# The last row group of the last down projection by column halves, each half added and stored on its own

## Chip, cores, metric

One core of one Trainium2 chip. The metric is the device time of the whole program in microseconds (us). The change acts on the last 4 us, so a second measure is used, the **tail**: from the start of the last matmul to the end of the span, read from the records of a trace.

## The reference

```python
x = A_u                                                    # [1, 2048, 640], bf16
h = x + _A_ref(_layernorm(x), ...)                         # a long convolution; not touched
h2 = h + _B_ref(_layernorm(h), B_w_gate, B_w_up, B_w_down) # 640 -> 1728 -> 640

def _B_ref(x, w_gate, w_up, w_down):
    g = jnp.einsum("bsd,df->bsf", x, w_gate)
    u = jnp.einsum("bsd,df->bsf", x, w_up)
    return jnp.einsum("bsf,fd->bsd", _sigmoid(g) * u, w_down)
```

## The kernel before

The sequence is worked on in four blocks (`b`) of 512 rows, each as four row groups (`lr`) of 128. For each block the down projection runs over two pairs of row groups (`lp` 0 and 2, `k` 0 and 1). A row group's 640 output columns are two halves (`c`) of 320, each in a PSUM bank. The two halves are slices of **one** tile `[P, 2, 512]`. In the last block the halves are added to `h` straight from PSUM and the row group is stored at once.

```python
        for lp in (0, 2):
            # ... (another pool setting, not in use)
                po = [[t[:, c] for c in range(2)] for t in (pso_p.tile([P, 2, 512], F32, name="ml_po", tag="ml_po") for _ in range(2))]

            def chunks(k, start, stop):
                lr = lp + k
                for ft in range(FT):                       # FT = 13
                    for c in range(2):
                        nc.tensor.matmul(po[k][c][:, 0:320], lhsT=hm[:, ft, 128 * lr:128 * lr + 128], rhs=Wd[:, ft, 320 * c:320 * c + 320],
                                         start=(start and ft == 0), stop=(stop and ft == FT - 1))
            # ... chunks(0), then the last 64 rows of both row groups side by side, then chunks(1)
            for k in range(2):
                lr = lp + k
                hv = hs[b][:, lr, :]
                h2 = hv.rearrange("p (c w) -> p c w", c=2)
                for c in range(2):
                    # ... (blocks 0 to 2 evict with ScalarE first)
                    nc.vector.tensor_tensor(h2[:, c], tb if b < NB - 1 else po[k][c][:, 0:320], h2[:, c], ALU.add)
                if b == NB - 1:
                    nc.sync.dma_start(oh[b, :, lr:lr + 1, :], hs[b][:, lr:lr + 1, :])
```

## Time and profile before

| | before |
|---|---|
| time | 356.66 us median of the first three runs (356.56 to 356.86) |
| span of the profiled run, granted clock | 355.0 us, 0.995 |
| tail | 3.87 us |

In the records of the trace, counted from the start of the last matmul, the tail goes like this: the first addition starts at 0.34, the second at 0.74, the store is issued at 1.25, its landing is seen at 3.05, the list of closing semaphore waits ends at 3.12, and the closing barriers take another 0.75. The prediction below shows the lines of the profile and how to read them.

### The profile page before, as it was taken

What the parts mean: (1) busy time and instruction counts of PE and PEld (TensorE: products, weight loads), DVE (VectorE), ACT (ScalarE), POOL (GpSimd) and SP (SyncE); (2) the same over time, 40 slices, a digit from 0 to 9 for tenths busy, and PEclk for the clock granted to TensorE, in tenths of its full rate; (3) what the DMA queues carried; (4) which work ended last, traced back from release to release, by engine and by line L of the source; (5) the groups of instructions that cost most, each with busy time, mean ns of one, the idle gap of its engine ahead of it and who ended that gap; (6) DMA issues with size and microseconds to landing.
All of it is one profiled execution on the core that took longest, in us unless ns stands there. A gap on an engine that the chain in (4) does not pass through costs nothing.

```text
span 355.0 us, 6617 instructions
## 1 busy us (share of the span) xinstructions
PE 320.4 (90%) x2584; PEld 204.0 (57%) x2584; DVE 283.3 (80%) x570; ACT 245.9 (69%) x455; POOL 11.4 (3%) x20
## 2 busy tenths in 40 slices
PE   2587989997799999899999899998899999999995
PEld 1464667765487778755456554555554456544463
DVE  3899999999898799879999899999899951211222
ACT  6999999998999764673767845547844678455500
POOL 1020002200000000100000100000100001000000
PEclk9998999999999999999999999999999999999999
DMA  6990000454205339989500053000012000400011
GB/s 172 323 404 4 15 2 2 113 179 157 76 3 160 137 88 352 289 273 280 227 4 0 5 179 113 3 0 0 3 74 76 0 1 11 133 7 1 0 37 38
DMA packets 32391, 35.00 MB, mean 99 GB/s; under 512 B 19676, under 2 KB 27741, under 8 KB 32104
## 3 DMA queue, kind: packets, MB, share of 16 engines
q1 hardware_dynamic: 32360, 34.59, 30.7%
q8 instruction: 20, 0.33, 0.4%
q14 instruction: 11, 0.09, 0.1%
HBM read 24.70 MB, written 9.21 MB: 96 GB/s over the span
## 4 chain that ended last, share of the span: by engine, by line
DVE 28%; PE 18%; issue 14%; ACT 2%; POOL 1%; POOLq 0%; DVEq 0%; ACTq 0%
DVE u L694 5%; PE ml_po L942 5%; DVE u L693 5%; PE ml_pg L909 5%; PE ml_pu L909 4%; DVE u L696 3%; DVE u L697 3%; DVE ml_hm L920 2%; DVE VR L704 2%; PE ps_y L565 1%; DVE Z L673 1%; DVE y L701 1%; DVE y L702 1%; DVE h L805 1%; ACT ln L859 1%
## 5 line engine op out<-in xcount | busy, mean ns | idle before, releaser
L909 PE MATMUL ml_pg<-lnT,Wg 128*128 128x512 bf16 x260 | 64.6, 379 | 0.2 <-ACT ml_sg L917 0.2
L909 PE MATMUL ml_pu<-lnT,Wu 128*128 128x512 bf16 x260 | 64.4, 379 | 0.0
L942 PE MATMUL ml_po<-Wd,ml_hm 128*128 128x320 bf16 x416 | 59.5, 299 | 1.7 <-ACT Wd L963 1.7
L942 PEld LDWEIGHTS <-ml_hm 128*128 128x128 bf16 x416 | 40.1, 98 | 19.6 <-issue 3.7
L917 ACT ACTIVATE ml_sg<-ml_pg 128x512 bf16<-128x512 f32 x52 | 30.9, 597 | 25.5 <-PE ml_pg L909 11.9
L920 DVE TENSOR_TENSOR ml_hm<-ml_ub,ml_sg 128x512 bf16<-128x512 bf16 x52 | 22.0, 423 | 28.0 <-ACT ml_ub L919 28.0
L909 PEld LDWEIGHTS <-Wu 128*128 128x128 bf16 x260 | 25.4, 98 | 30.7 <-issue 0.3
L919 ACT CAST ml_ub<-ml_pu 128x512 bf16<-128x512 f32 x52 | 30.4, 584 | 17.0 <-PE ml_pu L909 16.9
L909 PEld LDWEIGHTS <-Wg 128*128 128x128 bf16 x260 | 25.4, 98 | 28.8 <-issue 0.4
L457 PE MATMUL ps_z<-u,c_G 128*128 128x320 bf16 x192 | 30.3, 307 | 4.5 <-ACT zs L458 2.7
L518 PE MATMUL ps_xk<-kv,c_KM 128*128 128x160 bf16 x320 | 27.0, 232 | 1.8 <-ACT S L522 0.8
L693 DVE TENSOR_TENSOR u<-Z,S 128x1280 bf16<-128x1280 bf16 x34 | 27.8, 820 | 0.0
L694 DVE TENSOR_TENSOR u<-Z,S 128x1280 bf16<-128x1280 bf16 x34 | 27.8, 820 | 0.0
L457 PEld LDWEIGHTS <-c_G 128*128 128x128 bf16 x192 | 18.9, 99 | 13.7 <-issue 6.0
L518 PEld LDWEIGHTS <-c_KM 128*128 128x128 bf16 x320 | 23.5, 98 | 4.5 <-issue 3.5
L247 PE MATMUL ps_t<-fr,c_dg 128*128 128x160 f16 (+1 forms) x180 | 19.7, 240 | 4.9 <-DMA c_dg<-s4c_dg 4.1
L247 PEld LDWEIGHTS <-c_dg 128*128 128x128 f16 x180 | 14.9, 100 | 11.4 <-DMA c_dg<-s4c_dg 4.7
L697 DVE TENSOR_TENSOR u<-u,u 128x1280 bf16<-128x1280 bf16 x23 | 18.9, 821 | 0.1
L696 DVE TENSOR_TENSOR u<-u,u 128x1280 bf16<-128x1280 bf16 x23 | 18.9, 821 | 0.0
L476 PE MATMUL pk<-tabB,tabA 128*128 128x84 bf16 x320 | 16.1, 200 | 1.8 <-ACT kts L477 1.4
L477 ACT CAST kts<-pk 128x420 bf16<-128x420 f32 x32 | 15.9, 558 | 1.8 <-PE pk L476 1.8
L476 PEld LDWEIGHTS <-tabA 128*128 128x128 bf16 x320 | 14.3, 97 | 4.8 <-issue 3.3
(158 smaller groups left out, 546.1 us busy)
## 6 DMA issues: line engine op xcount, KB each, us to landing
dz<-zs SPq DMA_DIRECT2D x12, 320.0 KB, 2.4
c_KM<-s4c_KM SPq DMA_DIRECT2D x1, 2560.0 KB, 12.6
dxk<-xk SPq DMA_DIRECT2D x16, 160.0 KB, 3.8
h<-in_A_u_dram SPq DMA_DIRECT2D x4, 640.0 KB, 4.4
eo<-dz SPq DMA_DIRECT2D x4, 640.0 KB, 4.3
S<-dxk SPq DMA_DIRECT2D x4, 640.0 KB, 5.3
Wg<-in_B_w_gate_dram SPq DMA_DIRECT2D x4, 520.0 KB, 9.4
Wu<-in_B_w_up_dram SPq DMA_DIRECT2D x4, 520.0 KB, 8.5
```

The source lines that it names most:

```text
L247: MM(ps[:, a, q * w:q * w + w], lhsT=dg[:, dk, :], rhs=fr[:, src, i, o + oo:o + oo + w], start=False, stop=(q == m - 1 and i == 1))
L457: MM(ps[:, ri, 0:UH], lhsT=G[:, ft, 0 if b in EO else hf, ri, r, :], rhs=us[b][:, r, o:o + UH], start=(r == rr[0]), stop=(r == rr[-1]))
L476: MM(pk[:, i, :], lhsT=A[:, ri, g].rearrange("p e c -> p (e c)"), rhs=B[:, ri, :, 4 * g:4 * g + 4], start=(ri == 0), stop=(ri == 1))
L518: mm = MM(ps[:, hf, ri * W:ri * W + W], lhsT=KM[:, ft, hf, ri, KI[d] + q, :], rhs=kv[:, j, :], start=(q == 0), stop=(q == len(KD[d]) - 1)).ins
L693: V(t1, z, k[:, :, :, hs_], ALU.mult)
L694: V(t2, z, k[:, :, ::-1, hs_], ALU.mult)
L696: V(s1, s1, t1, ALU.add)
L697: V(s2, s2, t2, ALU.add)
L909: nc.tensor.matmul(ps[:], lhsT=W[:, dc, f0:f0 + 128], rhs=lnT[:, dc].rearrange("p a b -> p (a b)"), start=(dc == 0), stop=(dc == 4))
L917: nc.scalar.activation(sg[:], pg[:], AF.Sigmoid)
L919: nc.scalar.copy(ub[:], pu[:])
L942: nc.tensor.matmul(po[k][c][:, 0:320], lhsT=hm[:, ft, 128 * lr:128 * lr + 128], rhs=Wd[:, ft, 320 * c:320 * c + 320], start=(start and ft ...
```

## The change

The intent: the matmuls of the very last row group first complete the left 320 columns and then the right ones, so that the left half can be added and stored beside the right half's 13 matmuls. The core of the diff (the rest moves code into a function and adds branches for a setting that is not in use):

```diff
+            end = b == NB - 1 and lp
+
             def chunks(k, start, stop):
                 lr = lp + k
-                for ft in range(FT):
-                    for c in range(2):
-                        nc.tensor.matmul(...)
+                for ft, c in [(ft, c) for c in range(2) for ft in range(FT)] if end and k else [(ft, c) for ft in range(FT) for c in range(2)]:
+                    nc.tensor.matmul(...)
@@
                     nc.vector.tensor_tensor(h2[:, c], ...)
-                if b == NB - 1:
+                    if end and k:
+                        nc.sync.dma_start(oh[b, :, lr, 320 * c:320 * c + 320], hv[:, 320 * c:320 * c + 320])
+                if b == NB - 1 and not (end and k):
                     nc.sync.dma_start(oh[b, :, lr:lr + 1, :], hs[b][:, lr:lr + 1, :])
```

More of the change, by code (lines that the diff above doesn't have):

```diff
@@ L869, in turn @@
             return
-        if b and AT["PW"]:
+        if b and AT["PW"] == 1:
             pts = [pso[0].tile([P, 4, 4, 128], BF16, name="ml_pt", tag="ml_po") for _ in range(2)]
@@ L878, in turn @@
         for dc in range(5):
-            pt = psg_p.tile([P, 4, 128], BF16, name="ml_pt", tag="ml_pg")
+            pp, tag = (pso[1], "ml_pu") if b and AT["PW"] == 2 else (psg_p, "ml_pg")
+            pt = pp.tile([P, 4, 128], BF16, name="ml_pt", tag=tag)
             for i in range(4):
@@ L895, in mlp @@
     pso_p = sc.pool("ml_pso", bufs=2, space=PSUM)
-    pso.append(pso_p)
+    pso += [pso_p, psu_p]
     tc.cur_priority += int(AT["LATER"])
@@ L909, in up, with last_up @@
                 nc.tensor.matmul(ps[:], lhsT=W[:, dc, f0:f0 + 128], rhs=lnT[:, dc].rearrange("p a b -> p (a b)"), start=(dc == 0), stop=(dc == 4))
+        def last_up():
+            pg = psg_p.tile([P, 512], F32, name="ml_pg", tag="ml_pg")
+            for dc in range(5):
+                nc.tensor.matmul(pg[:], lhsT=Wl[:, dc].rearrange("p a b -> p (a b)"), rhs=lnT[:, dc].rearrange("p a b -> p (a b)"), start=(dc == 0), stop=(dc == 4))
+            sg = tmp.tile([P, 512], BF16, name="ml_sg")
+            nc.scalar.activation(sg[64:128, :], pg[0:64, :], AF.Sigmoid)
+            for k in range(2):
+                ev = lambda t: t.rearrange("p (a b c) -> p a b c", b=2, c=128)[:, :, k]
+                nc.vector.tensor_tensor(ev(hm[64 * k:64 * k + 64, FT, :]), ev(pg[64:128, :]), ev(sg[64:128, :]), ALU.mult)
         for ft in range(FT):
@@ L922, in mlp @@
                 drain(inv, 1)
-        pg = psg_p.tile([P, 512], F32, name="ml_pg", tag="ml_pg")
-        for dc in range(5):
-            nc.tensor.matmul(pg[:], lhsT=Wl[:, dc].rearrange("p a b -> p (a b)"), rhs=lnT[:, dc].rearrange("p a b -> p (a b)"), start=(dc == 0), stop=(dc == 4))
-        sg = tmp.tile([P, 512], BF16, name="ml_sg")
-        nc.scalar.activation(sg[64:128, :], pg[0:64, :], AF.Sigmoid)
-        for k in range(2):
-            ev = lambda t: t.rearrange("p (a b c) -> p a b c", b=2, c=128)[:, :, k]
-            nc.vector.tensor_tensor(ev(hm[64 * k:64 * k + 64, FT, :]), ev(pg[64:128, :]), ev(sg[64:128, :]), ALU.mult)
-        for lp in (0, 2):
-            if lp and AT["PW"]:
+        last_up()
+        for lp in (0, 2):
+            if lp and AT["PW"] == 2:
+                po = [[psg_p.tile([P, 512], F32, name="ml_po", tag="ml_pg") for _ in range(2)]]
+                t = pso_p.tile([P, 2, 512], F32, name="ml_po", tag="ml_po")
+                po.append([t[:, c] for c in range(2)])
+            elif lp and AT["PW"]:
                 po = [[p.tile([P, 512], F32, name="ml_po", tag=t) for _ in range(2)] for p, t in ((psg_p, "ml_pg"), (psu_p, "ml_pu"))]
@@ L936, in mlp @@
                 po = [[t[:, c] for c in range(2)] for t in (pso_p.tile([P, 2, 512], F32, name="ml_po", tag="ml_po") for _ in range(2))]
+            end = b == NB - 1 and lp
             def chunks(k, start, stop):
                 lr = lp + k
-                for ft in range(FT):
-                    for c in range(2):
-                        nc.tensor.matmul(po[k][c][:, 0:320], lhsT=hm[:, ft, 128 * lr:128 * lr + 128], rhs=Wd[:, ft, 320 * c:320 * c + 320],
+                for ft, c in [(ft, c) for c in range(2) for ft in range(FT)] if end and k else [(ft, c) for ft in range(FT) for c in range(2)]:
+                    nc.tensor.matmul(po[k][c][:, 0:320], lhsT=hm[:, ft, 128 * lr:128 * lr + 128], rhs=Wd[:, ft, 320 * c:320 * c + 320],
                                          start=(start and ft == 0), stop=(stop and ft == FT - 1))
```

## The prediction

> **What bounds the kernel now.** I read the page first, then the chain of waits over the last microseconds, then the timeline of the end, the waits of VectorE and of the store queue there, and last the list of DMA issues.
>
> The page says that this is a TensorE kernel, at full clock, and that nothing near the end disturbs it:
>
> ```profile
> span 355.0 us, 6617 instructions
> PE 320.4 (90%) x2584; PEld 204.0 (57%) x2584; DVE 283.3 (80%) x570; ACT 245.9 (69%) x455; POOL 11.4 (3%) x20
> PEclk9998999999999999999999999999999999999999
> ```
>
> The change touches only what happens after the last gate and up matmuls, so the whole-span shares say little. What counts is the chain that ends last, in its final five microseconds:
>
> ```profile
> 349.91 1.51 PE ml_po L942 x11
> 351.42 0.02 issue
> 351.44 0.49 DVE h L964
> 351.94 0.40 DVEq L1027
> ```
>
> The last matmul of the down projection ends at 351.42, and only then does VectorE begin on the last row group: one addition of 0.49 us and a second one whose end comes 0.40 us after it. The timeline of the end shows the same two additions as one entry, and the last store behind them:
>
> ```profile
> 347.70 3.71 PE L942 MATMUL ml_po<-Wd,ml_hm 128*128 128x320 bf16 x26
> 351.44 0.89 DVE L964 TENSOR_TENSOR h<-ml_po,h 128x320 bf16<-128x320 f32 x2 [2.75 <-PE ml_po L942]
> 352.36 0.33 SPq L966 DMA_DIRECT2D out_dram<-h  x1
> ```
>
> The bracket is the line to look at: VectorE sat idle for 2.75 us before the pair, waiting for TensorE. So VectorE has plenty of time to add the first column half early, if it were told that it is ready. The views of line L966 and of the last waits give the rest:
>
> ```profile
> DMA to landing us min/median/max: 1.8/1.8/2.3
> SPq L1027 <- DMA out_dram<-h: 1.1, 1, 1.1
> ```
>
> The tail after the last matmul is therefore: 0.02 wait, 0.89 of additions (to 352.33), 0.03 to the store's issue (352.36), 1.8 to its landing (about 354.2), and 0.8 of closing barriers to 355.0. That is 3.6 us, 1% of the span. No change confined to this tail can move the time by 2%, which is 7.1 us.
>
> **What the Trainium skill says.** (1) "PSUM — Partial Sum Buffer", section "Summary: rules for kernel authors", tells a kernel that wants to read PSUM while a matmul runs to aim at a different bank and to guard by bank. The output tile here is two halves of 512 f32 each, which that page's specifications give as one bank each, so the early addition is allowed; the trace of before has no such overlap within a row group. (2) "TensorE: Matmul & The Clock Gate", section "The mechanism", says that matmuls end strictly in the order of issue, so that one increment on the last is sound. The reverse matters here: who waits for the last one's increment waits for all. The trace agrees with it in so far as both additions of before follow the last matmul by 0.02 us. (3) "DMA: Bandwidth & Descriptors", section "Anatomy of one DMA — SWDGE (gpsimd) path", puts about 2.0 us of fixed cost on a DMA, mostly the receipt of the write, plus bytes over 436 GB/s. The trace agrees in form: a store of 160 KB lands in 1.8 us, and the view of the whole-block stores (L968, 640 KB) gives 2.9 us. The slope is 1.1 us for 480 KB (0.0023 us per KB, about 447 GB/s), and the fixed part 1.8 - 160 x 0.0023 = 1.43 us; smaller than the page's, on a queue of another kind. (4) The same page's "Specifications" ask for 512 B or more per transfer for the full rate. Before has runs of 1280 B per partition, the change 640 B, still above.
>
> **The change part by part.** Everything outside the last block's second pair of row groups is the same. I compared the two built programs instruction by instruction with source lines stripped: ACT and POOL are identical, TensorE has the same 5126 instructions of which only the last 26 loads and matmuls are in another order, VectorE has the same two additions, and the store queue has two instructions more. The new branches for other pool settings are dead, as the setting is still 0.
>
> *Matmuls.* Before, the 26 matmuls alternate between the halves; after, 13 go to the first and 13 to the second. The same 26 weight loads remain. Alternation or not should not matter: line L909 puts five matmuls in a row into one bank and takes 1.08 us for five in the chain, 216 ns for 512 columns, 0.42 ns a column; L942 alternates and takes 3.53 us for 26 (the first group in the chain), 136 ns for 320 columns, also 0.42 ns. So 0.0 us, and the last matmul still ends at 351.42.
>
> *Additions.* The intent is that the first half's addition runs beside the second half's 13 matmuls. The built program says it does not. In both programs only the very last matmul of this pair of halves increments TensorE's semaphore for this tile (by 27, to 2564), and the first half's addition waits for 2564 in both; the second half's addition waits for nothing of TensorE. If the wait followed each half, the second addition would need a wait of its own. It has none, so the dependence is held for the whole two-bank tile. The first addition therefore starts at 351.44 again, and the second at 351.85, 0.41 us later. Gain 0.0 us.
>
> *Stores.* The first half's store may now go after the first addition: 351.44 + 0.49 + 0.03 = 351.96, instead of 352.36. Its issue takes 0.33 us and then one small semaphore instruction (17 ns by the view of L966), so the queue is free at 352.31, just before the second addition's end at 352.33. The second store is issued at 352.36, the time of the only store before. It carries 80 KB in place of 160, so by the slope it lands 80 x 0.0023 = 0.18 us earlier. The first store's data begin 0.4 us earlier than before and take some 0.2 to 0.3 us, so they are off the engines as the second's begin. Smaller pieces do not scale perfectly, so I take 0.15 us of gain.
>
> *Closing waits.* At the end the queue goes through a list of semaphore waits. Before, the last store's semaphore is in the last of them; after, the second store uses another one, which stands third of six, with three more after it. The view of the closing line has these at 28 ns median each, so 3 x 0.028 = 0.08 us are walked after the landing instead of before it. Loss 0.08 us.
>
> Sum: 0.0 + 0.0 - 0.15 + 0.08 = -0.07 us. From the median of 356.66, 356.6 us.
>
> **The rivals.**
> *A: the addition is hidden after all*, because I misread the wait. Then 0.41 us of additions go from the tail and the second store is issued at about 351.95; with its smaller size the gain is 0.41 + 0.15 - 0.08 = 0.5 us, and the time 356.2. For it: the 2.75 us of idle VectorE, and the two halves in two banks. Against it: the wait values of the built program, which the hardware can't pass early. I give it 4%.
> *B: the second store is held up by the first*, in the issue or in the queue, where both are in flight together with twice the pieces. If the queue is late by a tenth or the first store's last writes have to be confirmed before the second's, the landing comes 0.1 to 0.4 us later than I said: 356.7 to 356.9. For it: the margin at the issue is only 0.02 us by the arithmetic above, and one of the four stores of L966 took 2.3 us to land without another in flight. Against it: the second half moves few bytes, and three of the four took 1.8. I give 25% to a result above 356.7 from this.
> *C: thirteen matmuls in a row into one bank are slower* than alternating ones. If each lost 10 ns, 26 x 0.01 = 0.26 us, and 356.9. Against it stands the equal time per column of L909 and L942. 3%.
>
> **Range and chances.** The mechanisms span 356.2 to 356.9; the three runs of before lie within 0.3 us of each other, and another set of runs may sit a few tenths off. That gives 356.2 to 357.0 for eight times in ten, centre 356.6. For 2% either way the time would have to leave 349.5 to 363.8, far outside what a 3.6 us tail can do; what is left is a surprise elsewhere in the program, though its instructions are the same. Faster 0.005, same 0.99, slower 0.005.
>
> **What would show each step right or wrong.** In the profile after, VectorE's last pair of additions should still be one entry of about 0.89 us behind the last matmul, with an idle time of about 2.75 us before it: then the split of the additions did nothing. If instead one addition stands near 349.6 (half way through the 26 matmuls) and a single one behind the last, rival A holds. The last 26 matmuls should take 3.7 us; 4.0 would be rival C. The store queue should show two issues 0.40 us apart, the second 0.94 us after the last matmul, with a landing of about 1.65 us against 1.8; 1.8 or more is rival B. From the last landing to the end of the span should be about 0.9 us instead of 0.8. The prediction is wrong if the time leaves its range, or if the first addition starts before the last matmul ends.

## The result

The changed kernel took 356.97 us (median of four runs, 356.35 to 357.59), the kernel before 356.62 us (four runs, 356.56 to 356.86). The ratio, 1.0008, has a 95% interval from 0.9989 to 1.0028: **the same**. Ratios in this text are not quite the ratio of the medians quoted.

The page of the changed kernel, its first lines and its clock line:

```profile
span 354.5 us, 6619 instructions
PE 320.6 (90%) x2584; PEld 205.0 (58%) x2584; DVE 283.4 (80%) x570; ACT 245.8 (69%) x455; POOL 11.4 (3%) x20
PEclk9999999999999999999999999999999999999999
```

The span is 0.43 us shorter than before. That is not a gain of the change: its chain of waits, over the end, shows that all of it was there before the last matmul ended (351.42 before, 350.96 now):

```profile
347.31 3.65 PE ml_po L951 x26
350.96 0.02 issue
350.98 0.49 DVE h L973
351.47 0.40 DVEq L1038
```

After that point the chain has the same pieces as before, to 0.01 us: matmuls 3.65, wait 0.02, an addition of 0.49, and the second addition's 0.40. The timeline of the end of the changed kernel:

```profile
350.98 0.89 DVE L973 TENSOR_TENSOR h<-ml_po,h 128x320 bf16<-128x320 f32 x2 [2.75 <-PE ml_po L951]
351.50 0.81 SPq L975 DMA_DIRECT2D out_dram<-h  x2
```

Both additions still stand behind the last matmul, and VectorE was idle for the same 2.75 us before them, although the left half's last matmul had started 13 matmuls earlier. Only the store has changed: two issues in 0.81 us. Their landing time, from the view of the store's line, and the semaphore waits of the closing line, first of the changed kernel:

```profile
DMA to landing us min/median/max: 1.6/1.6/1.6
L1038 SPq EVENT_SEMAPHORE  x8: 17/28/1097, 352.4 to 354.5; - x8
```

and of the kernel before:

```profile
L1027 SPq EVENT_SEMAPHORE  x8: 17/28/28, 352.7 to 354.9; - x8
```

In this view the three numbers are the shortest, median and longest duration in ns. The 1097 ns is the wait for the last store, now inside an entry that has further ones behind it.

In the records of the traces, from the last matmul's start, the landing of the last store is seen at 2.92 us (3.05 before), the list of closing waits ends at 3.15 (3.12), and the span at 3.90 (3.87). The smaller store brings 0.13 us, the list takes 0.16 us back, and the tail is 0.03 us longer.

### The profile page after: what moved, and what is told of

Read it like the earlier page. It is cut to its first block, busy times and chain, and to the rows that moved or that the text cites. A ratio compares the mean times of both kernels' runs of the same rounds, so it can differ in the third digit from the quotient of the medians.

```text
span 354.5 us, 6619 instructions
## 1 busy us (share of the span) xinstructions
PE 320.6 (90%) x2584; PEld 205.0 (58%) x2584; DVE 283.4 (80%) x570; ACT 245.8 (69%) x455; POOL 11.4 (3%) x20
## 4 chain that ended last, share of the span: by engine, by line
DVE 26%; PE 16%; issue 15%; SPq 3%; DMA 2%; ACT 1%; POOL 1%; POOLq 0%; DVEq 0%; ACTq 0%
DVE u L694 5%; PE ml_po L951 5%; DVE u L693 5%; PE ml_pg L910 5%; PE ml_pu L910 4%; DVE u L696 3%; DVE u L697 3%; DVE ml_hm L931 2%; DMA Wl<-in_B_w_gate_dram 2%; DVE VR L704 2%; SPq L822 2%; SPq L823 1%; DVE Z L673 1%; DVE y L701 1%; DVE y L702 1%
## 5 line engine op out<-in xcount | busy, mean ns | idle before, releaser
L457 PE MATMUL ps_z<-u,c_G 128*128 128x320 bf16 x192 | 29.2, 298 | 4.8 <-ACT zs L458 1.9
```

What stands on the lines that cost most here:

```text
L457: MM(ps[:, ri, 0:UH], lhsT=G[:, ft, 0 if b in EO else hf, ri, r, :], rhs=us[b][:, r, o:o + UH], start=(r == rr[0]), stop=(r == rr[-1]))
```

## The experiments

Nine runs were made, all with correct results: the first four on one chip with eleven runs of the kernel before, the next four on another chip with eleven new runs of it, and uneven_lastsem on that second chip too, with one more (its comparison uses all twelve). Each row of the table below comes from one trace; the tail of a kernel is compared, not its time, unless timed runs are quoted. A kernel without timed rounds has a single execution, whose state is unknown. All positions are us from the start of the last matmul, read from the traces' records; "landing seen" is where the wait for the last store's semaphore is over, "closing list ends" where the instruction behind the list starts.

| kernel | matmuls | PSUM tiles of the last row group | stores of it | 1st addition starts | 2nd starts | last store issued | landing seen | closing list ends | tail |
|---|---|---|---|---|---|---|---|---|---|
| before | alternate | one | 1 | 0.34 | 0.74 | 1.25 | 3.05 | 3.12 | 3.87 |
| after | halves | one | 2 | 0.34 | 0.75 | 1.28 | 2.92 | 3.15 | 3.90 |
| after_again | halves | one | 2 | 0.34 | 0.74 | 1.29 | 2.93 | 3.16 | 3.91 |
| order_only | halves | one | 1 | 0.34 | 0.75 | 1.26 | 3.05 | 3.12 | 3.87 |
| store_only | alternate | one | 2 | 0.34 | 0.75 | 1.29 | 2.93 | 3.16 | 3.92 |
| two_tiles | halves | two | 2 | -1.43 | 0.34 | 0.86 | 2.45 | 2.62 | 3.38 |
| two_tiles_one_store | halves | two | 1 | -1.43 | 0.34 | 0.86 | 2.66 | 2.72 | 3.48 |
| two_tiles_alt | alternate | two | 2 | 0.20 | 0.61 | 1.15 | 2.80 | 2.97 | 3.73 |
| after_lastsem | halves | one | 2 | 0.34 | 0.75 | 1.29 | 2.93 | 3.00 | 3.76 |
| two_tiles_lastsem | halves | two | 2 | -1.43 | 0.34 | 0.86 | 2.46 | 2.53 | 3.28 |
| uneven_lastsem | 384 + 256 | two | 2 | -1.11 | 0.31 | 0.76 | 2.32 | 2.38 | 3.14 |

**My theory** was: the order of the matmuls is idle, because the first addition waits for the whole two-bank tile; the split store acts, and the closing list takes its gain back. **The rivals**: the order costs or gives something by itself; an early addition would be worth nothing anyway; the split costs time that one trace does not show.

### after_again: is the 0.35 us in the medians real?

No edit. The changed kernel again, five more rounds.

> The changed kernel unchanged, to see whether the 356.97 us median against 356.62 us is a real loss. My theory: its tail (last matmul's start to the end of the span) is 3.90 us in its trace against 3.87 us before, so the time is the same within 0.1 us, ratio 1.000, and the spread 356.35 to 357.59 comes from the granted clock and the rest of the program. Rival: the split costs some 0.3 us that one trace does not show; then the ratio is 1.001 with an interval above 1.

356.77 us (six runs, 355.69 to 357.19) against 356.69 us (eleven runs, 356.13 to 357.32), ratio 0.9997, interval 0.9982 to 1.0012. The 0.35 us of the first medians did not repeat. The tail was 3.91 us. The spread has another place: in the traces the last matmul starts anywhere from 350.2 to 352.3 us, although the work before it is the same or all but the same. The granted clock alone does not order these: of the eleven traces the one with the earliest last matmul (store_only) has 0.995 and the one with the latest (two_tiles_lastsem) 1.0. What moves it was not looked into.

### order_only: the matmuls by halves, one store

```diff
-                    if end and k:
-                        nc.sync.dma_start(oh[b, :, lr, 320 * c:320 * c + 320], hv[:, 320 * c:320 * c + 320])
-                if b == NB - 1 and not (end and k):
+                if b == NB - 1:
```

> Matmuls by column halves, but one store of the whole row group. My theory: the wait of the first addition is for the whole two-bank tile, so the order of the matmuls changes nothing: tail 3.87 us as in the kernel before, VectorE idle 2.75 us before the last pair. Rival (the order itself matters, same-bank matmuls slower or the addition early): the last 26 matmuls take over 3.8 us, or the idle time falls below 2 us.

Timeline of its end:

```profile
347.88 3.71 PE L951 MATMUL ml_po<-Wd,ml_hm 128*128 128x320 bf16 x26
351.62 0.89 DVE L973 TENSOR_TENSOR h<-ml_po,h 128x320 bf16<-128x320 f32 x2 [2.75 <-PE ml_po L951]
```

The matmuls take 3.71 us as before, the idle time is 2.75 us as before, the tail 3.87 us as before. The order of the matmuls, alone, does nothing: neither good nor harm. Thirteen in a row into one bank are as fast as alternating ones.

### store_only: the old order, two stores

```diff
-                for ft, c in [(ft, c) for c in range(2) for ft in range(FT)] if end and k else [(ft, c) for ft in range(FT) for c in range(2)]:
+                for ft, c in [(ft, c) for ft in range(FT) for c in range(2)]:
```

> Matmuls in the old alternating order, but two stores. My theory: the same tail as the changed kernel, 3.90 us, as the split of the store is all of the change that acts: the landing about 0.13 us earlier, the closing waits about 0.16 us longer. Rival (order and store work together): a tail different from 3.90 us by over 0.05 us.

Timeline of its end:

```profile
350.56 0.89 DVE L973 TENSOR_TENSOR h<-ml_po,h 128x320 bf16<-128x320 f32 x2 [2.75 <-PE ml_po L951]
351.07 0.81 SPq L975 DMA_DIRECT2D out_dram<-h  x2
```

The tail is that of the changed kernel within 0.02 us (3.92), without its reordering. Together with order_only, this shows that the split store is all of the change that acts. Its single execution took 355.9 us; with the tail as it is, nothing is read from that.

### two_tiles: what the change meant to do

```diff
             end = b == NB - 1 and lp
+            if end:
+                po[1] = [psu_p.tile([P, 512], F32, name="ml_po", tag="ml_pu") for _ in range(2)]
```

The buffers that held the up projection are free by then. In the built program the waits now differ, which is the point of the edit. A semaphore is a counter: here TensorE raises it when matmuls are done, and an addition waits until it has reached a value. TensorE's semaphore, and the value that each of the last two additions waits for:

```
              first addition   second addition   increments among the last 26 matmuls
before, after      2564             none          at the 26th, to 2564
two_tiles          2551             2564          at the 13th, to 2551; at the 26th, to 2564
```

The traces bear this out: over the last 26 matmuls the changed kernel's records have one increment of this semaphore, 0.31 us after the last matmul's start, and those of two_tiles have two, 1.45 us before it and 0.31 us after it. Each addition that waits starts 0.02 us after its increment.

> The changed kernel with each half of the last row group in a PSUM tile of its own. My theory: now the first addition starts about 1.9 us before the last matmul ends and only one addition of 0.49 us stands behind it; the tail becomes 3.90 - 0.41 = 3.49 us, time ratio to before 0.999, about 0.4 us faster. Rival (the hidden addition is worth nothing as the store or a bank conflict takes its place): the tail stays at 3.8 us or more.

Timeline of its end:

```profile
347.84 3.71 PE L953 MATMUL ml_po<-Wd,ml_hm 128*128 128x320 bf16 x26
349.81 0.49 DVE L975 TENSOR_TENSOR h<-ml_po,h 128x320 bf16<-128x320 f32 x1 [0.99 <-PE ml_po L953]
350.33 2.10 SPq L977 DMA_DIRECT2D out_dram<-h  x2
351.58 0.49 DVE L975 TENSOR_TENSOR h<-ml_po,h 128x320 bf16<-128x320 f32 x1 [1.27 <-PE ml_po L953]
```

Now there are two entries of VectorE: the first addition starts 1.77 us before the second, in the middle of the matmuls, and the first store is issued at 350.33, long before the last matmul ends. The 26 matmuls still take 3.71 us, so reading one bank beside writing another cost them nothing. The tail fell to 3.38 us, 0.53 us under the changed kernel and 0.11 us better than the theory's 3.49. Some 0.06 us of the difference is a shorter closing list (two entries behind the landing instead of three, 0.16 instead of 0.22 us), another 0.04 us the landing itself: 1.60 us after the issue's start instead of 1.64. That difference lies in the issuing instruction, first of the changed kernel, then of two_tiles (shortest, median and longest in ns):

```profile
L975 SPq DMA_DIRECT2D out_dram<-h x2: 332/354/377, 351.5 to 351.9; - x2
L977 SPq DMA_DIRECT2D out_dram<-h x2: 332/332/333, 350.3 to 352.1; - x2
```

The second store's issue takes 377 ns in each of the five traces where it follows the first by 0.43 us, and 332 or 333 ns where it stands alone; from the end of the issue to the landing it is 1.26 us in both. Why the close neighbour's issue is longer was not looked into.

The time, 356.17 against 356.69 us, has a ratio of 0.999 (0.997 to 1.001): in the right direction, and not clear of the spread by itself.

### two_tiles_one_store and two_tiles_alt: which part of it carries the gain

```diff
 two_tiles_one_store
-                    if end and k:
-                        nc.sync.dma_start(oh[b, :, lr, 320 * c:320 * c + 320], hv[:, 320 * c:320 * c + 320])
-                if b == NB - 1 and not (end and k):
+                if b == NB - 1:
 two_tiles_alt
-                for ft, c in [(ft, c) for c in range(2) for ft in range(FT)] if end and k else ...:
+                for ft, c in [(ft, c) for ft in range(FT) for c in range(2)]:
```

> Halves in tiles of their own, in the order by halves, but one store of the whole row group. My theory: one addition behind the last matmul, the store issued 0.86 us after the last matmul's start as with two tiles, landing 1.79 us later as in the kernel before, closing waits as in the kernel before: tail 3.47 us, so that 0.40 of the 0.49 us come from the addition and the rest from the store. Rival (the split store carries the gain): tail near 3.87 us.

> Halves in tiles of their own and two stores, but the matmuls alternate as in the kernel before. My theory: the first half is complete only one matmul (0.136 us) before the second, so the first addition starts 0.2 us after the last matmul's start and the tail is about 3.67 us. Rival (the separate tiles alone do it): tail 3.38 us as with the order by halves.

Timeline of the end of two_tiles_one_store:

```profile
350.12 0.49 DVE L975 TENSOR_TENSOR h<-ml_po,h 128x320 bf16<-128x320 f32 x1 [0.99 <-PE ml_po L953]
351.88 0.49 DVE L975 TENSOR_TENSOR h<-ml_po,h 128x320 bf16<-128x320 f32 x1 [1.27 <-PE ml_po L953]
```

and of two_tiles_alt:

```profile
351.80 0.89 DVE L975 TENSOR_TENSOR h<-ml_po,h 128x320 bf16<-128x320 f32 x2 [2.62 <-PE ml_po L953]
352.32 0.81 SPq L977 DMA_DIRECT2D out_dram<-h  x2
```

With one store the tail is 3.48 us (expected 3.47): the hidden addition is worth 0.39 us against before. With two tiles but alternating matmuls, VectorE's idle time falls by just one matmul, from 2.75 to 2.62 us, and the additions are one entry again: tail 3.73 us. I had expected 3.67. The 0.05 us are in the second store: issued 0.43 us behind the first one, it lands 1.65 us after its issue, about as in the changed kernel (1.64), not 1.60 as alone. So hiding the addition needs both the order and the separate tiles. The order alone brings nothing (order_only). The tiles alone bring 0.19 us against store_only (3.73 against 3.92): about 0.14 us from additions that start one matmul earlier, and 0.06 us from the shorter closing list.

### after_lastsem: what the closing list takes

The program ends with a list of waits, among them those for the eight semaphores that the stores and loads take in turn. Storing row groups 0 and 1 together makes one transfer fewer, and the last store then has the semaphore that stands in the last entry of the list.

```diff
-                if b == NB - 1 and not (end and k):
-                    nc.sync.dma_start(oh[b, :, lr:lr + 1, :], hs[b][:, lr:lr + 1, :])
+                if b == NB - 1 and not end and k:
+                    nc.sync.dma_start(oh[b, :, 0:2, :], hs[b][:, 0:2, :])
+                if end and not k:
+                    nc.sync.dma_start(oh[b, :, lr:lr + 1, :], hs[b][:, lr:lr + 1, :])
```

> The changed kernel with the stores of row groups 0 and 1 as one, so that the last store gets the semaphore that the closing waits ask for last. My theory: the landing stays at 2.92 us after the last matmul's start, but 0.067 instead of 0.225 us pass from there to the end of the list: tail 3.74 us. Rival (the closing list costs nothing, or the small store lands as late as the large one): tail 3.87 us or more.

The waits of the closing line in its profile:

```profile
L1040 SPq EVENT_SEMAPHORE  x8: 17/28/28, 353.3 to 355.2; - x8
```

The 1097 ns entry is gone from the middle of the list. The landing is seen at 2.93 us as in the changed kernel, the list ends 0.07 us later instead of 0.22, and the tail is 3.76 us (expected 3.74): 0.14 us shorter than that of the changed kernel, and 0.11 us shorter than before. So the split store did have a gain of its own, and the closing list had swallowed it.

### two_tiles_lastsem: both

Edits of two_tiles and of after_lastsem.

> Both: halves in tiles of their own, two stores, and the last store on the semaphore that is asked for last. My theory: 3.375 us less 0.10 us of closing waits, a tail of 3.28 us; time ratio to before 0.998, some 0.6 us faster. Rival: the two gains do not add; tail 3.37 us.

Tail 3.28 us, as expected. Time 356.16 us (six runs, 356.06 to 357.36) against 356.99 us (eleven runs, 356.36 to 357.46), ratio 0.9985, interval 0.9972 to 0.9999: just clear of 1, and 0.59 us of tail are there to account for it.

### uneven_lastsem: less work behind the last matmul

As two_tiles_lastsem, with the last row group cut at column 384 in place of 320, in its matmuls, additions and stores:

```diff
+            even = ((0, 320), (320, 320))
+            cut = (even, ((0, 384), (384, 256)) if end else even)
```

> As two_tiles_lastsem, but the last row group is cut at column 384, so that 256 columns come last. My theory: the last addition is shorter by 64 columns, some 0.07 us, and the last store smaller by 16 KB, some 0.03 us; the 13 matmuls of 256 columns still take longer than a weight load of 98 ns, so TensorE loses nothing: tail 3.18 us. Rival (short matmuls are held up by their weight loads, or the smaller pieces cost the store its gain): 26 matmuls over 3.45 us from first to last start, or a tail of 3.28 us or more.

Timeline of its end:

```profile
350.02 0.56 DVE L981 TENSOR_TENSOR h<-ml_po,h 128x384 bf16<-128x384 f32 x1 [1.33 <-PE ml_po L956]
351.44 0.42 DVE L981 TENSOR_TENSOR h<-ml_po,h 128x256 bf16<-128x256 f32 x1 [0.86 <-PE ml_po L956]
```

The addition behind the last matmul takes 0.42 instead of 0.49 us, and the tail is 3.14 us (expected 3.18). As the last matmul is shorter here, a fairer start is the first of the 26 matmuls: from there to the end of the span it is 6.57 us, against 6.69 for two_tiles_lastsem, a gain of 0.12 us. From the first to the last of the 26 starts it is 3.43 us, under the rival's 3.45. Time 356.25 us (six runs) against 356.78 us (the twelve runs), ratio 0.9985 (0.9972 to 0.9999). It is the best tail, 0.73 us under before, or 0.70 us counted from the first of the 26 matmuls; the times do not tell it from two_tiles_lastsem.

## Why the prediction was right, by its steps

- **Same program but for the end: held.** The time is the same, and nothing ahead of the last row group moved that the run-to-run spread does not also move.
- **Matmuls, 0.0 us: held.** From the first to the last start of the 26 it is 3.406 us before and after; order_only repeats it.
- **Additions, 0.0 us: held, and its cause is shown.** The step was read from wait values, not from time. The idle time stayed at 2.75 us, and giving each half its own tile, the sole edit of two_tiles, moved the first addition by 1.77 us. That edit also takes the tiles from another pool; that the tile, and not the place, is what counts rests on the wait values and on the two increments in its trace. (The prediction's remark that both additions of before follow the last matmul by 0.02 us holds for the first; the second comes 0.41 us after the first.) Rival A (the addition is hidden after all) fell; its worth, which the prediction put at 0.41 us, was 0.39 us in two_tiles_one_store.
- **Stores, 0.15 us of gain: right in size, with a small loss that was named as rival B.** The store of half the size lands 1.64 us after its issue instead of 1.80, a gain of 0.16. But it was issued 1.28 us after the last matmul's start instead of 1.25, so 0.13 us came through. The prediction had the queue free 0.02 us before the second addition ends. In the trace it was free 0.03 us after that (1.255 against 1.225): between the first issue and the small semaphore instruction lie 0.05 us that the sum left out. Rival B's size of 0.1 to 0.4 us was too large: the near neighbour costs 0.03 us at the issue and some 0.04 us in the landing (1.64 against 1.60 alone), which is its longer issue. The first store's data took 0.39 us, not 0.2 to 0.3, yet were done 0.09 us before the second's began (2.07 and 2.16), as predicted.
- **Closing waits, 0.08 us of loss: too small by half.** The term was three entries by the 28 ns that the profile gives for one. But the first of them starts 37 ns after the landing is seen and the other two 62 and 59 ns after the one before, 0.16 us in all: from the landing to the end of the list the trace has 0.22 us after against 0.07 before. The duration of one entry was taken for the distance between two. So from the landing to the end of the span it was 0.98 us, not the predicted 0.9, against 0.82 before. This term (0.08 us) and the 0.02 us missing from the stores turned the sum from -0.07 into +0.03 us; after_lastsem, which takes the term away, gets a tail 0.11 us under before.
- **Rival C (one bank in a row is slower)** fell with order_only.

That the time fell into the range was partly luck. The sum had the wrong sign, though only by 0.10 us, and the range, set in part by the spread of three runs, proved wide enough only narrowly: the median, 356.97, lies 0.03 us under its upper end, and two of the four single runs lie above it. Eleven runs of the kernel before spread over 1.2 us, four times what those three had shown. What is confirmed is the mechanism, by the tails; the 0.37 us between the predicted 356.6 and the median lie within the spread, and after_again did not repeat them.

## What to carry to other kernels

Work that is to be released piece by piece needs its pieces apart for whatever tracks dependences, not only in the order of the instructions: here two slices of one tile were released together, and two tiles one by one. Before a run, compare the waits and increments of the built programs: a consumer that has no wait of its own tells that its forerunner waits for both. At the very end of this program halving the last store was worth 0.1 to 0.2 us (after_lastsem against before, two_tiles_lastsem against two_tiles_one_store) and the place of its semaphore in the closing list 0.09 to 0.14 us, which shows only in a trace and not in times that spread over a microsecond.

## What the Trainium skill lacked or had wrong

- "Perfetto Trace Analysis", section "Sequencer-only Instruction (DRAIN, etc)", says that the profiler leaves the wait for a semaphore out of an instruction's reported time. Here that depends on where the semaphore stands in an entry that waits for two: as the first of the two, the last store's wait was left out (28 ns before), as the second it was inside (1097 ns after, 1092 ns in two_tiles). All eleven traces follow this, the six and the five of each kind.
- The same section speaks of a hidden tail on each such instruction without a size. In the closing list here an entry is reported with 28 ns, and the next starts 62 ns after its start.
- "DMA: Bandwidth & Descriptors", section "Anatomy of one DMA — SWDGE (gpsimd) path", fits about 2.0 us of fixed cost for the path of GpSimd, and that page has no such fit for stores from SyncE. Here, from issue to landing: 1.60 us for 80 KB alone, 1.64 us for 80 KB issued 0.43 us behind another, 1.80 us for 160 KB, 2.9 us for 640 KB.
- No page that I read has a cost for the place of the last store's semaphore in a program's closing list; the runs show 0.16 us for three entries behind it.
